# Turned probabilities of both heads in one tile, joint copies for the two small chunks and the packed rows, and one inversion of a pair's nine sums

## The chip, the cores and the metric

The kernel runs on one core of one Trainium2 chip. The metric is the device time of one execution in microseconds. Three runs of the kernel before took 829.68, 830.39 and 831.4 us, median 830.39. One more execution was profiled; its own time was 829.02 us, and its span, from the first to the last recorded instruction, 827.3 us.

The engines are called PE (matrix products and transposes; PEld is its loading of weights, which overlaps the products), DVE, ACT, POOL and SP. Each runs its own instructions in their order and waits on semaphores for the others. The large transfers are issued from SP's queue.

## The reference

First causal attention over 8 batches, 8 heads, 576 positions and a head size of 64, with a bias that is the difference of running sums; its output is then the input of a mixture of 8 experts, of which each token takes one.

```python
s_pos = np.maximum(s, 0.0)
cum = np.cumsum(s_pos, axis=-1)
bias = -(cum[:, :, :, None] - cum[:, :, None, :])
scores = np.where(causal, -1000000000.0, scores + np.minimum(bias, 0.0))
scores = scores - np.max(scores, axis=-1, keepdims=True)
attn = np.exp(scores)
attn = attn / (np.sum(attn, axis=-1, keepdims=True) + 1e-09)
return np.matmul(attn, v).astype(np.float32)
...
h = np.maximum(x[mask] @ w1[e], 0.0)
out[mask] = gate_w[mask, None] * (h @ w2[e])
```

There are 4608 tokens of 512 numbers; an expert has 1024 hidden units.

## The kernel before

**Tiling.** Attention works on 32 pairs. A pair is one head of two batches; the code calls the two `ab` 0 and 1, and the title calls them both heads. The 576 queries of each are cut in four chunks of 128 and a rest of 64; the rests of both batches are packed into one chunk of 128 rows. So a pair has nine chunks: `i` from 0 to 7 (`ab = i // 4`, chunk `c = i % 4` with `128 * (c + 1)` keys), and `i = 8`, the packed rows, with 576 keys. They are taken in the order 3, 7, 2, 6, 8, 1, 5, 0, 4 (`ORDER`).

**A chunk's way.** PE makes the scores in two products into one bank `sp` (four buffers): `KA` by `QH` (L373) and `KB` by `QL` (L395); the packed rows take L408 and L409 in two halves of 288 keys. DVE adds the mask, takes the minimum and writes `pe` or `pep` to SBUF (L397, L411). ACT takes the exponential in place, with the row's sum into `sums` (L417). Three steps later (`LAG`) PE turns the probabilities in blocks of 128x128 into a PSUM tile `pt` (L427; packed rows L440), of which there are **two buffers**, and a copy puts them into `PT` in SBUF: ACT at L430 for `i < 8`, DVE at L446 for the packed rows. The fifth block of the packed rows goes to a corner of the tile `o`.

**A pair's end.** `tail` runs twice. With `g = 1`: PE multiplies the turned probabilities of the queries from 256 on by V (L467, 20 products in all); this needs the chunks 2 and 3 and the packed rows. ACT and DVE copy the result into `oT` (L470, L474), PE projects it by `pw` and `pq` (L347), and DVE scales it by the inverted sums `rs` (L489, L491). With `g = 0` the same is done for the queries 0 to 255, that is chunks 0 and 1. `rs` is made by an addition on ACT (L479) and a reciprocal on DVE (L480), once for each `g`.

**Order of the work.** The loop in `run` writes steps in program order, one chunk per step, and the turning of chunk k - 3 behind the scores of chunk k. A scheduler then fixes the order on each engine from its own estimates; some `issue_after` edges hold it. POOL makes the exact high and low parts of the next pair's keys and queries meanwhile. After every eighth pair `done` routes the tokens that are complete: the sums of the gate columns (L670, DVE) and what follows run in the steps `QUIET` of the next pairs.

**Experts.** From about 380 us on PE multiplies gathered tokens by the expert weights (L1081, L1056) to the end.

**Tiles that the change touches.** `PT`: three tiles of 128x1984, of which a pair takes two in turn. `oT`: two tiles. `pe`: six buffers of 128x512. `V`: three buffers, loaded one pair ahead.

Of the kernel before, what the change touches and what calls it, by code (L numbers as in the profile page):

```python
# [7 lines left out]
F32 = mybir.dt.float32  # L8
# [3 lines left out]
AF = mybir.ActivationFunctionType  # L12
ALU = mybir.AluOpType
# [24 lines left out]
class Attn:  # L38
# [3 lines left out]
    def __init__(self, ctx, tc, qkv, s, ident, wg):  # L42
        nc = tc.nc
# [10 lines left out]
        self.QL = [t[:, :1280].rearrange("p (a x) -> p a x", a=2) for t in self.QLx]  # L54
        self.KA = [c.tile([P, 2, KW], F32R, name=f"KA{u}") for u in range(2)]
        self.KB = [c.tile([P, 2, KW], F32R, name=f"KB{u}") for u in range(2)]
        self.PT = [c.tile([P, PTW], F32, name=f"PT{u}") for u in range(3)]
        self.oT = [c.tile([P, 640], F32, name=f"oT{u}") for u in range(2)]
        self.pw = c.tile([P, 8, 2 * XW], F32, name="pw")
        self.pq = c.tile([P, 8, XW], F32, name="pq")  # L60
        self.mk = c.tile([P, 800], F32, name="mk")
# [4 lines left out]
        self.hold, self.act, self.sp = [None], None, None  # L66
        self.t1 = ExitStack()
        t1 = self.t1p = self.t1.enter_context(tc.tile_pool(name="cst", bufs=1, side="right"))
        sr = t1.tile([P, KW], F32, name="sr")
        for k in HALVES:  # L70
            nc.sync.dma_start(sr[:, k], s[:, k])
        raw = self.raws()
# [18 lines left out]
        s8 = t1.tile([P, KW], F32, name="s8")  # L91
# [198 lines left out]

    def consts(self):
        nc = self.nc
        for u in range(2):
            nc.gpsimd.memset(self.oT[u][:, 512:], 0.0)
        for t in self.PT:
            nc.vector.memset(t[64:, PTW - 64:], 0.0)

    def raws(self):
        return [self.ld.tile([P, 2, KW], F32, name="rawq"), self.ld.tile([P, 2, KW], F32, name="rawk")]
# [6 lines left out]
        return raw  # L306

    def load_v(self, pi):
        V = self.ld.tile([P, 2, 5, 64], F32, name="V", bufs=3)
        self.nc.sync.dma_start(V, self.qkv[pi, :, 4 * KW:].rearrange("p (a j d) -> p a j d", a=2, j=5))  # L310
        return V

# [63 lines left out]
    def score(self, st, i):  # L376
        nc = self.nc
# [4 lines left out]
        if i < 8:  # L382
# [1 line left out]
            n = P * (c + 1)  # L384
            nn = max(n, 256)
            q0 = 704 * ab + P * c
            t = self.wk.tile([P, 512], F32, name="pe", bufs=6)
            if st["pi"] == 0 and not st["s"]:

                for j in ORDER[:SPB]:  # L390
# [27 lines left out]

    def trans(self, st, i):
        nc = self.nc  # L420
        pe, PT = st["s"].pop(i), st["PT"]
        cp = nc.vector.tensor_copy if i in PTDVE else nc.scalar.copy
        if i < 8:
            ab, c = i // 4, i % 4
            pt = self.ps1.tile([P, 512], F32, name="pt")
            for j in range(c + 1):
                self.pe.append(nc.tensor.transpose(out=pt[:, P * j:P * j + P], in_=pe[:, P * j:P * j + P], identity=self.ident).ins)  # L427
            v = min(P * c, 320)
            w = PT[ab][:, P * c - v:P * c - v + PTS * (c + 1)].rearrange("p (j s) -> p j s", s=PTS)
            cp(w[:, :, v:v + P], pt[:, :P * (c + 1)].rearrange("p (j q) -> p j q", q=P))  # L430
        else:
            for j0, nj in ((0, 4), (4, 1)):
                if nj == 4:
                    pt = self.ps1.tile([P, 512], F32, name="pt")
                else:
                    st["o"] = self.ps2.tile([P, 512], F32, name="o")
                    pt = st["o"][:64, 384:]
                kp = P if nj == 4 else 64
                for j in range(nj):
                    self.pe.append(nc.tensor.transpose(out=pt[:kp, P * j:P * j + P], in_=pe[:, P * (j0 + j):P * (j0 + j) + kp], identity=self.ident).ins)  # L440
                for ab in range(2):
                    if nj == 4:
                        w = PT[ab][:, 128:128 + 4 * PTS].rearrange("p (j s) -> p j s", s=PTS)[:, :, 384:]
                    else:
                        w = PT[ab][:kp, PTW - 64:].unsqueeze(1)
                    cp(w, pt[:kp, :P * nj].rearrange("p (j a q) -> p a j q", a=2, q=64)[:, ab])  # L446

    def tail(self, st, g):

        nc = self.nc  # L450
        V, PT, x, h = st["V"], st["PT"], st["x"], st["h"]
        for _ in range(TD + g):
            yield
        q0, q1 = (256, KW) if g else (0, 256)
        o = st["o"] if g else self.ps2.tile([P, 512], F32, name="o")
        oT = self.oT[st["pi"] % 2]

        pe, self.pe = self.pe, []
        nj = 5 if g else 2
        for j in range(nj):  # L460
            f = max(P * j, q0)
            for ab in range(2):
                r = slice(64 * ab, 64 * ab + 64)
                with ExitStack() as after:
                    for i in pe:
                        after.enter_context(self.tc.issue_after(i))
                    m = nc.tensor.matmul(o[r, f - q0:q1 - q0], V[:, ab, j, :], PT[ab][:, PTS * j + f if j < 4 else PTW - 64:PTS * j + q1 if j < 4 else PTW], start=j == 0, stop=j == nj - 1)  # L467
            pe = [m.ins]
        self.wall = m.ins
        nc.scalar.copy(oT[:, q0:q0 + 256], o[:, :256])  # L470
        if g:
            for ab in range(2):
                r = slice(64 * ab, 64 * ab + 64)
                nc.vector.tensor_copy(oT[r, 512 + 64 * ab:576 + 64 * ab], o[r, 256:320])  # L474
        yield
        n = 5 if g else 4
        rs = self.sm.tile([P, 5], F32, name="rs")
        with self.tc.issue_after(self.hold[0]), self.tc.issue_after(self.act):
            nc.scalar.activation(rs[:, :n], st["sums"][:, 4 * g:4 * g + n], AF.Identity, bias=self.eps[:, :1])  # L479
            nc.vector.reciprocal(rs[:, :n], rs[:, :n])  # L480
        xo = self.xo
        for u in range(2):
            c = 2 * g + u
            self.pw_(xo[:, 2 * XW * u:2 * XW * u + 2 * XW], oT[:, P * c:P * c + P], self.pw[:, h, :], start=True, stop=True)
        if g:
            self.pw_(xo[:, 4 * XW:5 * XW], oT[:, 512:], self.pq[:, h, :], start=True, stop=True)
        src = xo[:, :4 * XW].rearrange("p (t d) -> p t d", t=4)
        rv = rs[:, :4].unsqueeze(2).broadcast_to([P, 4, XW])
        nc.vector.tensor_tensor(x[g][:, :, :, h], src.rearrange("p t (d r) -> p t d r", r=2), rv.rearrange("p t (d r) -> p t d r", r=2), ALU.mult)  # L489
        if g:  # L490
            nc.vector.tensor_scalar(x[2][:, 0, :, h], xo[:, 4 * XW:5 * XW].rearrange("p (d r) -> p d r", r=2), rs[:, 4:5], None, ALU.mult)  # L491

    def run(self, npair, newx, done, setup):

# [4 lines left out]
        for k in range(n + LAG + 9):  # L499
            if k < n:  # L500
# [885 lines left out]
```

## Time and profile before

| | |
|---|---|
| median of three runs | 830.39 us (829.68 to 831.4) |
| profiled execution | 829.02 us, its span 827.3 us |
| PE busy | 812.1 us, 98% of the span |
| DVE, ACT busy | 545.6 us (66%), 541.3 us (65%) |
| POOL busy | 360.5 us (44%) |

The page lists busy time by engine; the view by windows gives it by stretch; the timeline lists instructions with start and length, in brackets the idle time just ahead of them and what ended it. Consecutive matmuls overlap in the records (a product of 0.48 us can be followed by the next after 0.31 us), so PE can stand as busy while it waits. What a wait costs is then read from the distance of the starts, not from the busy time.

### The profile page before, as it was taken

Reading aid. Unit: us, or ns where it says so; the run is one execution under the profiler, and the core shown is the slowest. Engines: PE = TensorE matmul, PEld = TensorE weight load, DVE = VectorE, ACT = ScalarE, POOL = GpSimd, SP = SyncE. Lnnn points to the kernel's source line nnn. Section 1 sums busy time; section 2 is a strip of 40 time slices with the busy share of each in tenths; the row PEclk is TensorE's granted clock in tenths of the full one; section 3 lists DMA queues with packets and bytes.
Section 4 is the critical chain, followed back from the end, with each engine's and each line's share of the span. In section 5 each row is a group of like instructions: output and inputs, shape, how many; then the busy total and the mean of one; then the engine's idle time right before and its main releaser. Section 6 shows DMA issues by size and latency. Waiting matters only on the chain. (4 is left out here: it accounts for less than half of the span.)

```text
span 827.3 us, 16879 instructions
## 1 busy us (share of the span) xinstructions
PE 812.1 (98%) x5692; PEld 695.5 (84%) x5692; DVE 545.6 (66%) x1502; ACT 541.3 (65%) x1292; POOL 360.5 (44%) x384
## 2 busy tenths in 40 slices
PE   7999999999999999999999999999999999999997
PEld 6778877877887878887888899998888999988884
DVE  7666667667666677766489865555666656555874
ACT  6788888888888888885365554444455555444663
POOL 8959768988689867992501000000000000000001
PEclk9999999999999999999999999999999999999999
DMA  7665555866567657738697866655556776555970
GB/s 238 187 195 180 180 179 181 254 223 195 170 182 230 208 155 213 226 97 288 222 381 291 312 259 257 229 202 197 213 201 244 258 258 243 199 202 207 380 247 28
DMA packets 68549, 182.31 MB, mean 220 GB/s; under 512 B 7993, under 2 KB 8889, under 8 KB 68334
## 3 DMA queue, kind: packets, MB, share of 16 engines
q1 hardware_dynamic: 62622, 161.17, 57.5%
q0 software_dynamic: 5840, 20.06, 6.3%
q8 instruction: 45, 0.74, 0.4%
q14 instruction: 42, 0.34, 0.1%
HBM read 144.73 MB, written 26.80 MB: 207 GB/s over the span
## 5 line engine op out<-in xcount | busy, mean ns | idle before, releaser
L1067 POOL DMA_INDIRECT out<-ys,oi x36 | 36.5, 1015 | 368.6 <-ACT ys L1066 297.5
L397 DVE CUSTOM_DVE_ANT_0 pe<-sp,mk 128x512 f32<-128x512 f32 (+3 forms) x256 | 121.2, 487 | 63.2 <-PE sp L395 55.5
L417 ACT ACTIVATE pe<-pe,mx 128x512 f32<-128x512 f32 (+3 forms) x256 | 143.8, 562 | 22.4 <-DVE mx L397 21.0
L427 PE MATMUL pt<-ident,pe 128*128 128x128 f32 x640 | 117.7, 281 | 4.0 <-ACT PT L430 2.8
L430 ACT COPY PT<-pt 128x512 f32<-128x512 f32 (+3 forms) x256 | 106.3, 416 | 13.3 <-PE pt L427 12.6
L1083 ACT ACTIVATE hT<-hp 128x512 fp32r<-128x512 f32 x72 | 42.8, 595 | 93.1 <-PE hp L1081 92.6
L467 PE MATMUL o<-PT,V 128*64 128x320 f32 (+4 forms) x896 | 100.7, 364 | 0.0
L373 PE MATMUL sp<-KA,QH 128*128 128x256 f32 (+2 forms) x256 | 97.3, 389 | 2.5 <-POOL KA L236 2.5
L427 PEld LDWEIGHTS pt<-ident,pe 128*128 128x128 f32 x640 | 75.4, 141 | 26.8 <-ACT PT L430 11.2
L467 PEld LDWEIGHTS o<-PT,V 128*64 128x64 f32 x896 | 58.7, 136 | 41.0 <-issue 9.4
L1081 PE MATMUL hp<-xT,wcb 128*128 128x256 f32 x648 | 89.6, 282 | 0.0
L395 PE MATMUL sp<-KB,QL 76*128 76x256 f32 (+2 forms) x256 | 88.4, 349 | 0.0
L1081 PE MATMUL hp<-xT,wca 128*128 128x256 f32 x624 | 87.3, 282 | 0.5 <-ACT xT L1033 0.5
L327 POOL TENSOR_TENSOR KA<-rawk,KA 64x576 fp32r<-64x576 f32 x62 | 87.0, 1419 | 0.2
L327 POOL TENSOR_TENSOR QL<-rawq,QH 64x576 fp32r<-64x576 f32 x62 | 86.6, 1413 | 0.2
L1084 DVE SCALAR_TENSOR_TENSOR hT<-hp,hT 128x512 fp32r<-128x512 f32 x72 | 49.5, 687 | 55.1 <-ACT hT L1083 54.9
L1081 PEld LDWEIGHTS hp<-xT,wcb 128*128 128x128 f32 x648 | 83.1, 188 | 0.6
L1081 PEld LDWEIGHTS hp<-xT,wca 128*128 128x128 f32 x624 | 80.4, 188 | 1.4 <-issue 0.7
L1056 PE MATMUL y<-wcb,hT 128*128 128x512 f32 x336 | 81.2, 398 | 0.0
L1056 PEld LDWEIGHTS y<-wcb,hT 128*128 128x128 f32 x336 | 62.7, 188 | 14.7
L1081 PE MATMUL hp<-xT,wcc 128*128 128x256 f32 x456 | 64.6, 281 | 0.0
L1056 PE MATMUL y<-wca,hT 128*128 128x512 f32 x264 | 63.9, 398 | 0.0
(285 smaller groups left out, 1611.9 us busy)
## 6 DMA issues: line engine op xcount, KB each, us to landing
wrbw<-in_w SPq DMA_DIRECT2D x104, 512.0 KB
wraw<-in_w SPq DMA_DIRECT2D x56, 512.0 KB
rawq<-in_qkv SPq DMA_DIRECT2D x31, 576.0 KB
rawk<-in_qkv SPq DMA_DIRECT2D x31, 576.0 KB
xg<-lists SPq DMA_DIRECT2D x18, 576.0 KB
V<-in_qkv SPq DMA_DIRECT2D x32, 320.0 KB
KB<-KA SPq DMA_DIRECT2D x62, 144.0 KB
lists<-z SPq DMA_DIRECT2D x8, 576.0 KB
```

The source lines that it names most:

```text
L327: self.last = nc.gpsimd.tensor_tensor(o, i, h, ALU.subtract).ins
L373: self.pe.append(self.nc.tensor.matmul(sp[:, :nn], QH[:, q0:q0 + P], self.KA[u][:, ab, :nn], start=True, stop=False).ins)
L395: self.pe.append(nc.tensor.matmul(sp[:, :nn], QL[:EXT, q0:q0 + P], KB[:EXT, ab, :nn], start=False, stop=True).ins)
L397: ins = nc.vector.tensor_tensor_reduce(out=t[:, :n], in0=sp[:, :n], in1=self.mk[:, 512 - n:512], scale=-0.125, scalar=3.0e38, op0=ALU.add, ...
L417: self.act = nc.scalar.activation(t[:, :n], t[:, :n], AF.Exp, bias=m, scale=-1.0, accum_out=st["sums"][:, o:o + 1]).ins
L427: self.pe.append(nc.tensor.transpose(out=pt[:, P * j:P * j + P], in_=pe[:, P * j:P * j + P], identity=self.ident).ins)
L430: cp(w[:, :, v:v + P], pt[:, :P * (c + 1)].rearrange("p (j q) -> p j q", q=P))
L467: m = nc.tensor.matmul(o[r, f - q0:q1 - q0], V[:, ab, j, :], PT[ab][:, PTS * j + f if j < 4 else PTW - 64:PTS * j + q1 if j < 4 else PTW], ...
L1056: self.last[0] = nc.tensor.matmul(y[u], hT[:, a, f, P * u:P * u + P], W[4 + f // 2][:, c, 512 * (f % 2):512 * (f % 2) + 512], start=f == 0 ...
L1081: nc.tensor.matmul(hp[:, u], W[k][:, a, f:f + P], xT[:, c, k], start=k == 0 and i == 0, stop=k == 3 and i == 2)
L1083: hi = nc.scalar.activation(hs, hp, AF.Relu)
L1084: lo = nc.vector.scalar_tensor_tensor(hT[:, 1, 2 * m:2 * m + 2], hp, 0.0, hs.bitcast(F32), ALU.max, ALU.subtract)
```

## The change

`PT` becomes two tiles of `[128, 2, 1984]`, one for each pair in turn, with both `ab` in one tile. That lets one copy serve both: for the chunks 0 and 1 (`JOINT`) the turning of `ab = 0` is left until that of `ab = 1`, both go into one `pt`, and ACT makes one copy of 128x2x2x128 or 128x2x128 in place of two. The packed rows take one DVE copy in place of two, and so does their corner in `o`. `rs` has nine columns and is made once a pair, with `g = 1`. `oT` becomes a single tile, `pe` gets a tile of its own width for each chunk length, with two buffers, `V` has two buffers and its load is written three steps later, and the two scratch tiles of the start lie inside `PT[1]`.

```diff
+JOINT = (0, 1)
...
-        self.PT = [c.tile([P, PTW], F32, name=f"PT{u}") for u in range(3)]
-        self.oT = [c.tile([P, 640], F32, name=f"oT{u}") for u in range(2)]
+        self.PT = [c.tile([P, 2, PTW], F32, name=f"PT{u}") for u in range(2)]
+        self.oT = c.tile([P, 640], F32, name="oT")
...
-        sr = t1.tile([P, KW], F32, name="sr")
+        sr, s8 = (self.PT[1][:, 0, KW * u:KW * u + KW] for u in range(2))
...
-        V = self.ld.tile([P, 2, 5, 64], F32, name="V", bufs=3)
+        V = self.ld.tile([P, 2, 5, 64], F32, name="V")
...
-            t = self.wk.tile([P, 512], F32, name="pe", bufs=6)
+            t = self.wk.tile([P, n], F32, name=f"pe{c}")
...
-        pe, PT = st["s"].pop(i), st["PT"]
+        PT = st["PT"]
         cp = nc.vector.tensor_copy if i in PTDVE else nc.scalar.copy
+        if i in JOINT:
+            return
         if i < 8:
             ab, c = i // 4, i % 4
+            both = i - 4 in JOINT
             pt = self.ps1.tile([P, 512], F32, name="pt")
-            for j in range(c + 1):
-                self.pe.append(nc.tensor.transpose(out=pt[:, P * j:P * j + P], in_=pe[:, P * j:P * j + P], identity=self.ident).ins)
+            n = P * (c + 1)
+            for a in range(1 - both, 2) if ab else (0,):
+                pe = st["s"].pop(4 * a + c)
+                for j in range(c + 1):
+                    o = n * (a if both else 0) + P * j
+                    self.pe.append(nc.tensor.transpose(out=pt[:, o:o + P], in_=pe[:, P * j:P * j + P], identity=self.ident).ins)
...
+            cp(w[:, :, :, v:v + P], pt[:, :n * (1 + both)].rearrange("p (a j q) -> p a j q", a=1 + both, q=P))
...
-                for ab in range(2):
-                    if nj == 4:
-                        w = PT[ab][:, 128:128 + 4 * PTS].rearrange("p (j s) -> p j s", s=PTS)[:, :, 384:]
-                    else:
-                        w = PT[ab][:kp, PTW - 64:].unsqueeze(1)
-                    cp(w, pt[:kp, :P * nj].rearrange("p (j a q) -> p a j q", a=2, q=64)[:, ab])
+                if nj == 4:
+                    w = PT[:, :, 128:128 + 4 * PTS].rearrange("p a (j s) -> p a j s", s=PTS)[:, :, :, 384:]
+                    cp(w, pt[:, :512].rearrange("p (j a q) -> p a j q", a=2, q=64))
+                else:
+                    cp(PT[:kp, :, PTW - 64:], pt[:kp, :P].rearrange("p (a q) -> p a q", a=2))
...
-        n = 5 if g else 4
-        rs = self.sm.tile([P, 5], F32, name="rs")
-        with self.tc.issue_after(self.hold[0]), self.tc.issue_after(self.act):
-            nc.scalar.activation(rs[:, :n], st["sums"][:, 4 * g:4 * g + n], AF.Identity, bias=self.eps[:, :1])
-            nc.vector.reciprocal(rs[:, :n], rs[:, :n])
+        if g:
+            rs = st["rs"] = self.sm.tile([P, 9], F32, name="rs")
+            with self.tc.issue_after(self.hold[0]), self.tc.issue_after(self.act):
+                nc.scalar.activation(rs, st["sums"], AF.Identity, bias=self.eps[:, :1])
+                nc.vector.reciprocal(rs, rs)
+        rs = st["rs"]
...
-                if k % 9 == 2 and 0 < pi < npair - 1:
+                if k % 9 == 5 and 0 < pi < npair - 1:
                     self.V[pi + 1] = self.load_v(pi + 1)
```

In the changed kernel the lines stand elsewhere: the turning of `i < 8` is L433 and its copy L437, that of the packed rows L448 and its copies L451 and L453, the scores are L372 and L394, the products by V L474, and the projections L346.

The scheduler orders the engines anew. The three places that the prediction speaks of follow. The rows name line, operation, tile written and tiles read, and the shape.

PE in a pair of the middle of attention, from the turning of chunk 6 (the first L427 row) to the products by V, before:

```order
L427 MATMUL pt<-ident,pe 128x128 x3
L395 MATMUL sp<-KB_108,QL_104 128x256
L440 MATMUL o<-ident,pep 64x128
L373 MATMUL sp<-KA_106,QH_102 128x256
L395 MATMUL sp<-KB_108,QL_104 128x256
L373 MATMUL sp<-KA_105,QH_101 128x512
L440 MATMUL pt<-ident,pep 128x128 x4
L395 MATMUL sp<-KB_107,QL_103 128x512
L373 MATMUL sp<-KA_105,QH_101 128x512
L427 MATMUL pt<-ident,pe 128x128 x2
L395 MATMUL sp<-KB_107,QL_103 128x512
L427 MATMUL pt<-ident,pe 128x128 x2
```

and changed:

```order
L394 MATMUL sp<-KB_108,QL_104 128x256
L433 MATMUL pt<-ident,pe_2440 128x128 x3
L372 MATMUL sp<-KA_106,QH_102 128x256
L394 MATMUL sp<-KB_108,QL_104 128x256
L448 MATMUL o<-ident,pep 64x128
L372 MATMUL sp<-KA_106,QH_102 128x256
L448 MATMUL pt<-ident,pep 128x128 x4
L394 MATMUL sp<-KB_108,QL_104 128x256
L372 MATMUL sp<-KA_105,QH_101 128x512
L394 MATMUL sp<-KB_107,QL_103 128x512
L433 MATMUL pt<-ident,pe_2481 128x128 x2
L433 MATMUL pt<-ident,pe_2498 128x128 x2
```

The turning of the chunks 1 and 5 (the last two rows) is one group now, with one `pt`, and one KA and KB product of 512 that stood ahead of it follows it. The turning of the packed rows (L440, now L448) stands ahead of one KB product of 256 and one KA product of 512 that it followed before, and that of chunk 6 is one KA product of 256 earlier.

DVE where the first routing begins, before (`PT<-pt` are the copies of the packed rows, L670 the sums of the gate columns, ISA the mask and minimum):

```order
L480 RECIPROCAL rs<-rs 128x4
L446 COPY PT_110<-o 64x64
L489 TENSOR_TENSOR x<-ox,rs 128x144x2
L446 COPY PT_111<-o 64x64
L670 TENSOR_REDUCE ox<-x 128x32
L446 COPY PT_110<-pt 128x4x64
L670 TENSOR_REDUCE ox<-x 128x32
L446 COPY PT_111<-pt 128x4x64
```

and changed:

```order
L497 TENSOR_TENSOR x<-ox,rs 128x144x2
L678 TENSOR_REDUCE ox<-x 128x32
L396 ISA pe_1690,mx<-sp,mk 128x256
L396 ISA mx 128x1
L678 TENSOR_REDUCE ox<-x 128x32
L396 ISA pe_1702,mx<-sp,mk 128x128
L396 ISA mx 128x1
L453 COPY PT_109<-o 64x2x64
L451 COPY PT_109<-pt 128x2x4x64
```

The two sums no longer stand between the copies but ahead of them, between the chunks.

DVE around the copies into `oT` behind the products by V, before:

```order
L474 COPY oT_112<-o 64x64 x2
L397 ISA pe,mx<-sp,mk 128x384
L397 ISA mx 128x1
```

and changed:

```order
L396 ISA pe_2266,mx<-sp,mk 128x384
L396 ISA mx 128x1
L481 COPY oT<-o 64x64 x2
```

The copies stand behind the mask of the next pair's chunk 2 now. On PE the product by `pq` that reads them follows one KA and one KB product of 384 and one turning that came behind it before.

More of the change, by code (lines that the diff above doesn't have):

```diff
@@ L90, in __init__ @@
         self.warm(WARM)
-        s8 = t1.tile([P, KW], F32, name="s8")
         for k in HALVES:
@@ L292, in consts @@
         nc = self.nc
-        for u in range(2):
-            nc.gpsimd.memset(self.oT[u][:, 512:], 0.0)
+        nc.gpsimd.memset(self.oT[:, 512:], 0.0)
         for t in self.PT:
-            nc.vector.memset(t[64:, PTW - 64:], 0.0)
+            nc.vector.memset(t[64:, :, PTW - 64:], 0.0)
     def raws(self):
@@ L361, in start @@
     def start(self, pi, x):
-        st = dict(pi=pi, h=pi % 8, x=x, s={}, high={}, PT=[self.PT[(2 * pi + ab) % 3] for ab in range(2)], V=self.V.pop(pi))
+        st = dict(pi=pi, h=pi % 8, x=x, s={}, high={}, PT=self.PT[pi % 2], V=self.V.pop(pi))
         st["mx"] = self.sm.tile([P, 10], F32, name="mx")
@@ L420, in trans @@
         nc = self.nc
-        pe, PT = st["s"].pop(i), st["PT"]
+        PT = st["PT"]
         cp = nc.vector.tensor_copy if i in PTDVE else nc.scalar.copy
+        if i in JOINT:
+            return
         if i < 8:
             ab, c = i // 4, i % 4
+            both = i - 4 in JOINT
             pt = self.ps1.tile([P, 512], F32, name="pt")
-            for j in range(c + 1):
-                self.pe.append(nc.tensor.transpose(out=pt[:, P * j:P * j + P], in_=pe[:, P * j:P * j + P], identity=self.ident).ins)
+            n = P * (c + 1)
[4 more added lines that the diff above has]
+                    self.pe.append(nc.tensor.transpose(out=pt[:, o:o + P], in_=pe[:, P * j:P * j + P], identity=self.ident).ins)
             v = min(P * c, 320)
-            w = PT[ab][:, P * c - v:P * c - v + PTS * (c + 1)].rearrange("p (j s) -> p j s", s=PTS)
-            cp(w[:, :, v:v + P], pt[:, :P * (c + 1)].rearrange("p (j q) -> p j q", q=P))
+            h = slice(0, 2) if both else slice(ab, ab + 1)
+            w = PT[:, h, P * c - v:P * c - v + PTS * (c + 1)].rearrange("p a (j s) -> p a j s", s=PTS)
+            cp(w[:, :, :, v:v + P], pt[:, :n * (1 + both)].rearrange("p (a j q) -> p a j q", a=1 + both, q=P))
         else:
+            pe = st["s"].pop(i)
             for j0, nj in ((0, 4), (4, 1)):
@@ L455, in tail @@
         o = st["o"] if g else self.ps2.tile([P, 512], F32, name="o")
-        oT = self.oT[st["pi"] % 2]
+        oT = self.oT
         pe, self.pe = self.pe, []
@@ L466, in tail @@
                         after.enter_context(self.tc.issue_after(i))
-                    m = nc.tensor.matmul(o[r, f - q0:q1 - q0], V[:, ab, j, :], PT[ab][:, PTS * j + f if j < 4 else PTW - 64:PTS * j + q1 if j < 4 else PTW], start=j == 0, stop=j == nj - 1)
+                    m = nc.tensor.matmul(o[r, f - q0:q1 - q0], V[:, ab, j, :], PT[:, ab, PTS * j + f if j < 4 else PTW - 64:PTS * j + q1 if j < 4 else PTW], start=j == 0, stop=j == nj - 1)
             pe = [m.ins]
@@ L487, in tail @@
         src = xo[:, :4 * XW].rearrange("p (t d) -> p t d", t=4)
-        rv = rs[:, :4].unsqueeze(2).broadcast_to([P, 4, XW])
+        rv = rs[:, 4 * g:4 * g + 4].unsqueeze(2).broadcast_to([P, 4, XW])
         nc.vector.tensor_tensor(x[g][:, :, :, h], src.rearrange("p t (d r) -> p t d r", r=2), rv.rearrange("p t (d r) -> p t d r", r=2), ALU.mult)
         if g:
-            nc.vector.tensor_scalar(x[2][:, 0, :, h], xo[:, 4 * XW:5 * XW].rearrange("p (d r) -> p d r", r=2), rs[:, 4:5], None, ALU.mult)
+            nc.vector.tensor_scalar(x[2][:, 0, :, h], xo[:, 4 * XW:5 * XW].rearrange("p (d r) -> p d r", r=2), rs[:, 8:9], None, ALU.mult)
     def run(self, npair, newx, done, setup):
```

## The prediction

> **What bounds the kernel now.** I read the page's busy times, then the view by windows, then the weight loads' waits, then the timeline of single pairs. Page and windows (us, busy time and count of each engine, granted clock, DMA):
>
> ```profile
> span 827.3 us, 16879 instructions
> PE 812.1 (98%) x5692; PEld 695.5 (84%) x5692; DVE 545.6 (66%) x1502; ACT 541.3 (65%) x1292; POOL 360.5 (44%) x384
> ...
> 160.00:320.00 160.00, 159.42 (x1260) 128.42 (x1259) 110.13 (x476) 133.73 (x438) 130.88 (x129) 1.00 0.64 196
> 400.00:800.00 400.00, 400.00 (x2582) 362.66 (x2582) 255.59 (x347) 206.74 (x260) 38.92 (x39) 1.00 0.69 252
> ```
>
> PE is the bound in both halves: 159.42 of 160 us in attention, 400 of 400 in the experts. ACT, whose work the change cuts most, is busy 133.73 of 160 us there (84%) and waits for PE in between. So the change is worth what it takes from PE's stalls, and since the experts are PE from end to end, each microsecond by which attention ends sooner should be kept to the end. These stalls hardly show as idle time; the weight loads' waits from 60 to 370 us show where they sit (sum, times, longest):
>
> ```profile
> PEld pt L427 <- ACT PT L430: 7.2, 30, 0.5
> PEld pt L427 <- PE pt L427: 4.2, 15, 0.3
> ```
>
> The turned tile `pt` has two buffers, and the turning waits until a copy has emptied one. These 11.4 us overlap running products in part, so they bound from above what this wait can cost there. One pair closely, PE first, then DVE, then the pair before it, PE:
>
> ```profile
> 159.22 0.38 PE L427 MATMUL pt<-ident,pe 128*128 128x128 f32 x2
> ...
> 159.85 0.41 PE L427 MATMUL pt<-ident,pe 128*128 128x128 f32 x2
> 160.19 2.27 PE L467 MATMUL o<-PT,V 128*64 128x320 f32 x20
> ...
> 158.95 0.75 DVE L446 COPY PT<-pt 128x256 f32<-128x256 f32 x2
> ...
> 148.04 0.38 PE L427 MATMUL pt<-ident,pe 128*128 128x128 f32 x2
> ...
> 148.49 0.40 PE L395 MATMUL sp<-KB,QL 76*128 76x512 f32 x1
> 148.72 0.38 PE L427 MATMUL pt<-ident,pe 128*128 128x128 f32 x2
> 149.04 0.76 PE L467 MATMUL o<-PT,V 128*64 128x320 f32 x4
> ```
>
> At 148 us nothing is late: two turnings and a product of 512 take 0.45 us (148.04 to 148.49), a product of 512 alone up to the next turning 0.23, and the turning takes 0.32 to the products by V. At 159 the same stretch takes 0.63 and 0.34: 0.20 us lost. It ends with the second copy of the packed rows (158.95 + 0.75 = 159.70; the turning starts 0.15 later, which is what a release takes to become a start). That is the stall of an ordinary pair: 0.20 of the 11.15 us from one product by V (149.04) to the next (160.19).
>
> **The change part by part.** PE's own work stays the same, product by product; only stalls can change.
>
> *Ordinary pairs, what goes.* The turning of chunk 5 no longer waits for the packed rows' second copy: its tile is now that of chunk 6, which ACT empties before. 0.20 us goes.
>
> *Ordinary pairs, what comes.* The order on PE puts the packed rows' turning (`pep`) and chunk 6's earlier. In the kernel before, the pair whose products by V start at 149.04 has nearly this order already and shows the price, PE and then ACT:
>
> ```profile
> 145.47 0.49 PE L427 MATMUL pt<-ident,pe 128*128 128x128 f32 x3
> 145.72 0.36 PE L373 MATMUL sp<-KA,QH 128*128 128x256 f32 x1
> 145.92 0.28 PE L395 MATMUL sp<-KB,QL 76*128 76x256 f32 x1
> 146.03 0.54 PE L427 MATMUL pt<-ident,pe 128*128 128x128 f32 x3
> 146.32 0.36 PE L373 MATMUL sp<-KA,QH 128*128 128x256 f32 x1
> ...
> 146.88 0.28 PE L395 MATMUL sp<-KB,QL 76*128 76x256 f32 x1
> 147.08 0.66 PE L440 MATMUL pt<-ident,pep 128*128 128x128 f32 x4
> 147.49 0.48 PE L373 MATMUL sp<-KA,QH 128*128 128x512 f32 x1
> ...
> 146.36 0.29 ACT L479 ACTIVATE rs<-sums,eps 128x4 f32<-128x4 f32 x1
> 146.55 0.47 ACT L430 COPY PT<-pt 128x384 f32<-128x384 f32 x1
> ```
>
> Chunk 6's turning takes 0.29 us where chunk 2's takes 0.25: 0.04 lost. `pep` starts 0.20 behind a product of 256 that otherwise takes 0.11 (145.92 to 146.03), and takes 0.41 where four turnings at the rate of three (0.25 / 3 each) take 0.33 and, with a first one that is always a little longer, say 0.36: 0.09 and 0.05, together 0.14 lost. It waits for ACT's copy of chunk 2 (146.55 + 0.47 = 147.02). That is 0.18 in all, so this order alone gains next to nothing over 0.20. In the changed kernel `pep` is one product of 256 (0.11) earlier still, and the copy it waits for is earlier by the `rs` that is gone ahead of it (146.55 - 146.36 = 0.19). So 0.14 + 0.11 - 0.19 = 0.06 at `pep`; with 0.04 at chunk 6, 0.10. Bounds: 0 if ACT comes sooner still; 0.04 + 0.14 + 0.11 = 0.29 if ACT's chain doesn't move up.
>
> The `pq` product comes on top. On DVE the copies into `oT` now stand behind a mask of 384 columns, and on PE `pq` stands behind two products of 384 and a turning more:
>
> ```profile
> L397 DVE CUSTOM_DVE_ANT_0 pe<-sp,mk 128x384 f32<-128x384 f32 x28 | 15.6, 557 | 7.4 <-PE sp L395 7.0
> 163.67 0.42 PE L373 MATMUL sp<-KA,QH 128*128 128x384 f32 x1
> 164.11 0.60 PE L427 MATMUL pt<-ident,pe 128*128 128x128 f32 x4
> ```
>
> The copies are later by up to 0.56, `pq` by 164.11 - 163.67 = 0.44 and a turning of about 0.09. A stall between 0 and 0.12; I take 0.06. The new sum is 0.16 against 0.20, a gain of 0.04 a pair (bounds: 0.20 less 0, and 0.20 less 0.41, so +0.20 to -0.21).
>
> *The larger copies.* A joint ACT copy is longer than a single one, and the packed DVE copy too. Neither has a row; these bound them:
>
> ```profile
> L430 ACT COPY PT<-pt 128x512 f32<-128x512 f32 x28 | 15.8, 564 | 0.0
> L430 ACT COPY PT<-pt 128x256 f32<-128x256 f32 x30 | 10.9, 363 | 3.2 <-PE pt L427 3.1
> ```
>
> On ACT, 512 columns take 0.56 in place of 2 x 0.36, off the path. On DVE the copy lies between one of 256 and the two, which take 0.75; I take 0.65, so V's products get the packed rows no later than before. The V load, one pair ahead by its issue, and the smaller buffers cost nothing by this reckoning: a pair's V lands while the 11 us of the pair before run.
>
> *The pair behind each of three group ends.* There L670 stands between the two packed copies (the order above), and the second copy is later by its length:
>
> ```profile
> 204.01 0.48 PE L395 MATMUL sp<-KB,QL 76*128 76x512 f32 x1
> 204.72 0.44 PE L427 MATMUL pt<-ident,pe 128*128 128x128 f32 x2 [0.23 <-ACT PT L430]
> 205.09 0.49 PE L467 MATMUL o<-PT,V 128*64 128x320 f32 x2
> ```
>
> 0.71 + 0.37 against 0.31 (0.45 less the 0.14 of the two turnings ahead) + 0.32: 0.45 lost. With the sums ahead of the copies I give it the ordinary 0.16, a gain of 0.29; the two pairs behind, where routing still crowds DVE, I put at 0.1 together for the group. Three groups: 1.2 us (bounds 0 and 2).
>
> *The first four pairs.* There chunk 5's turning directly follows chunk 1's, both buffers in use:
>
> ```profile
> 23.02 0.41 PE L427 MATMUL pt<-ident,pe 128*128 128x128 f32 x2 [0.47 <-DVE PT L446]
> 34.33 0.38 PE L427 MATMUL pt<-ident,pe 128*128 128x128 f32 x2
> 34.98 0.41 PE L427 MATMUL pt<-ident,pe 128*128 128x128 f32 x2 [0.27 <-DVE PT L446]
> 46.37 0.44 PE L427 MATMUL pt<-ident,pe 128*128 128x128 f32 x2 [0.46 <-ACT PT L430]
> 58.18 0.44 PE L427 MATMUL pt<-ident,pe 128*128 128x128 f32 x2 [0.46 <-ACT PT L430]
> ```
>
> At 34 us the two starts are 0.65 apart where two turnings take about 0.22, so 0.43 is lost, 0.16 more than the idle time in brackets, because the record of a turning outlasts its slot. With 0.16 added to each the four lose 2.3 us. One joint tile cannot wait for itself; less 4 x 0.16 of the ordinary new stalls, the gain is 1.7 (bounds 0.8 and 2.3).
>
> *The last pair* has the same two waits:
>
> ```profile
> 372.75 0.44 PE L427 MATMUL pt<-ident,pe 128*128 128x128 f32 x2 [0.21 <-ACT PT L430]
> 373.64 0.44 PE L427 MATMUL pt<-ident,pe 128*128 128x128 f32 x2 [0.46 <-ACT PT L430]
> 374.01 0.76 PE L467 MATMUL o<-PT,V 128*64 128x320 f32 x4
> ```
>
> With the joint tile the four turnings start at 372.75 and V's products about 0.4 to 0.55 later, at 373.2 to 373.3: 0.7 us (bounds 0.3 and 0.9).
>
> *The sum.* 32 pairs less 4, 3 and 1 are 24 ordinary ones: 24 x 0.04 = 1.0; with 1.2, 1.7 and 0.7 it is 4.6 us. 829.02 - 4.6 = 824.4 for a profiled execution (1.7 us of it around the span, which the change leaves alone); the median lies 1.4 above that execution, so 825.8.
>
> **A rule that speaks against the change.** The Trainium skill, page "Perfetto Trace Analysis", section "Optimizing Scalar/DVE Operations", says that grouping into larger operations can pay where the engine is saturated, and that where it isn't but makes others wait, breaking instructions up may let work finish sooner. ACT at 84% and DVE at 69% of the attention window (133.73 and 110.13 of 160) are of the second kind, and PE waits for both. The trace agrees with both halves of its condition. By this rule alone the joint copies lose; the slower rival below is that case.
>
> **The rivals.**
>
> *No change.* PE's stalls only move: new waits of 0.25 a pair take the place of 0.20. For it: the pair at 145 us, whose new order gains nothing. Against: its `rs` at 146.36, which goes. 24 x -0.05 = -1.2, group ends 0, start 2.3 - 4 x 0.25 = 1.3, end 0.7: a gain of 0.8, 829.6.
>
> *Slower: `pep` waits for the tile of chunk 2.* Its place moved ahead of a KA product of 512 and a KB product of 256, and if ACT's chain ahead of that copy is paced by DVE's masks of the packed rows rather than by ACT's own length, dropping `rs` moves nothing. Then 0.29 at `pep` and chunk 6 and 0.12 at `pq`: 0.41, a loss of 0.21 a pair. 24 x 0.21 = 5.0, nothing at the group ends, against 2.3 - 4 x 0.41 = 0.7 at the start and 0.7 at the end: 3.6 slower, 834.0. It decides from a new stall of 0.28 a pair on, where 24 pairs lose as much as start and end gain, and from 0.34 on a measurement would tell it. For it: ACT is idle in 26 of the window's 160 us, so it isn't always the pace. Against: from 145 us on, `rs` and the copy run back to back on ACT.
>
> *All stalls go.* 24 x 0.20 = 4.8, with 2.0, 2.3 and 0.9: 10.0, 820.4. Against: chunk 6's wait has no reason to go.
>
> *ACT sets the pace.* A pair saves 2 x 0.36 - 0.56 = 0.16 at each of two joint copies and 0.19 of `rs`: about 0.5, 31 pairs 16 us, 814. Against: PE at 159.42 of 160.
>
> **How the numbers follow.** Forecast 0.52, no change 0.21, slower 0.15, all stalls gone 0.11, ACT's pace 0.01. A measurement tells about 0.2% (1.7 us) from no change. The forecast's own range is 823 to 828.5 (a gain of the ordinary pair of 0.14, and of -0.07), wholly on the faster side of 828.7; the forecast, the last two and a little of the second give faster 0.66, same 0.19, slower 0.15. The range runs from 821.0 to 831.5: below it lies some 0.08, above it the larger part of the slower case.
>
> **What would show it.** Right: the distance between V's first products of ordinary pairs falls from 11.15 to about 11.11; no bracketed idle time at the joint turning in the first pairs and the last; waits of the weight load for `pt` fall from 11.4 to some 6 us and move to `pep`; the experts' stretch keeps its length. Wrong: `pep` starting over 0.2 us behind the KA product ahead of it, or `pq` waiting for `oT` in every pair, or an experts' stretch that grows by what attention gave.

## The result and the profile after

The changed kernel took 833.25 us (median of 8 runs, 831.71 to 835.18) against 829.77 us of the kernel before (8 runs, 829.05 to 831.4): a ratio of 1.0043, 95% interval 1.0031 to 1.0055. It is slower by 3.5 us where 4.6 us of gain were forecast. The profiled execution took 832.43 us.

The page's first lines and its windows after (columns as before):

```profile
span 830.6 us, 16652 instructions
PE 814.3 (98%) x5692; PEld 698.1 (84%) x5692; DVE 539.6 (65%) x1405; ACT 530.5 (64%) x1196; POOL 360.3 (43%) x383
...
40.00:60.00 20.00, 17.34 (x132) 13.77 (x130) 11.13 (x45) 13.60 (x43) 14.01 (x18) 1.00 0.64 186
60.00:80.00 20.00, 19.69 (x138) 14.89 (x140) 11.28 (x44) 14.21 (x42) 13.78 (x19) 0.91 0.49 157
...
160.00:320.00 160.00, 160.00 (x1266) 130.55 (x1266) 107.56 (x433) 129.84 (x398) 133.16 (x131) 1.00 0.66 202
400.00:800.00 400.00, 400.00 (x2582) 362.72 (x2581) 255.00 (x348) 206.28 (x260) 41.48 (x41) 1.00 0.69 252
```

ACT has 11 us less to do and DVE 6, as the change says, and PE has none of it. One place stands out: from 40 to 60 us PE is busy for 17.34 of 20 us. The kernel before has this row there:

```profile
40.00:60.00 20.00, 19.07 (x146) 14.86 (x146) 13.22 (x57) 16.25 (x52) 10.50 (x10) 1.00 0.68 217
```

The starts of V's first product in each pair, read from the timeline, say which pairs it is (us from one to the next; the pairs are counted from 0):

| pair | 1 | 2 | 3 | 4 | 5 | ordinary | last |
|---|---|---|---|---|---|---|---|
| before | 11.50 | 11.88 | 11.82 | 11.17 | 11.17 | 11.17 | 11.34 |
| changed | 11.23 | 12.32 | 14.53 | 12.27 | 11.61 | 11.16 | 10.54 |

By the start of pair 5's product the changed kernel is 4.2 us behind (85.58 against 81.35, the first and second row below); at the last pair's it is 2.6 behind (376.59 against 374.01), so 1.7 came back between. The experts' products take the same time, to 0.03 us, and the last write lands 0.7 later behind the last product (7.1 us against 6.4; other runs here have 6.5 to 6.9).

```profile
81.35 0.49 PE L467 MATMUL o<-PT,V 128*64 128x320 f32 x2
```
```profile
85.58 0.49 PE L474 MATMUL o<-PT,V 128*64 128x320 f32 x2
```

What PE waits for there, in the view of waits from 34 to 86 us of the changed kernel, and the timeline of PE (timelines are shown here and below with rows in between left out):

```profile
PE sp L372 <- POOL KA L326: 3.1, 5, 1.9
...
58.94 0.50 PE L372 MATMUL sp<-KA,QH 128*128 128x512 f32 x1 [1.91 <-POOL KA L326]
60.31 0.61 PE L372 MATMUL sp<-KA,QH 128*128 128x512 f32 x1 [0.43 <-POOL KA L326]
```

PE waits for POOL's low part of the next pair's keys. POOL in turn starts late. The chain is on SP's queue; first the kernel before, POOL and then SP (SPq rows are the issue of transfers):

```profile
33.87 1.31 POOL L323 TENSOR_SCALAR KA<-rawk 128x576 fp32r<-128x576 f32 x2 [0.45 <-DMA rawk<-in_qkv]
...
26.24 0.57 SPq L310 DMA_DIRECT2D V<-in_qkv  x1
26.87 0.44 SPq L305 DMA_DIRECT2D rawq<-in_qkv  x1
...
33.57 0.57 SPq L262 DMA_DIRECT2D KB<-ek  x1
```

and the changed kernel, with SP's waits from 20 to 85 us:

```profile
37.67 1.31 POOL L322 TENSOR_SCALAR KA<-rawk 128x576 fp32r<-128x576 f32 x2 [4.75 <-PE sp L394]
...
30.28 0.33 SPq L309 DMA_DIRECT2D V<-in_qkv  x1
30.66 0.42 SPq L304 DMA_DIRECT2D rawq<-in_qkv  x1
...
37.03 0.57 SPq L262 DMA_DIRECT2D KB<-ek  x1
...
SPq L309 <- PE o L474: 10.0, 3, 3.9
```

The load of V stands at the same place of the queue in both. With three buffers it goes out at once; with two it has to wait until PE has multiplied by the V of the pair before last, and three such loads wait 10.0 us in all. Behind it stand the raw keys and queries, the rows that are saved to DRAM (five transfers that take some 5 us to issue) and the next pair's placements into KB and QL. They all go out 3.5 to 4 us later, and so does what POOL makes of them: it starts 6.5 us behind the issue of the raw keys in both kernels (27.35 to 33.87 and 31.14 to 37.67), though the second row names a product of PE as what ended the wait.

The ordinary pair, at last, in the timelines of PE, ACT and DVE of the changed kernel:

```profile
186.93 2.27 PE L474 MATMUL o<-PT,V 128*64 128x320 f32 x20
190.78 0.44 PE L346 MATMUL ox<-pq,oT 128*128 128x72 f32 x2
192.55 0.87 PE L474 MATMUL o<-PT,V 128*64 128x256 f32 x8
196.00 0.66 PE L448 MATMUL pt<-ident,pep 128*128 128x128 f32 x4
197.09 0.60 PE L433 MATMUL pt<-ident,pe 128*128 128x128 f32 x4
198.09 0.76 PE L474 MATMUL o<-PT,V 128*64 128x320 f32 x4
...
195.48 0.47 ACT L437 COPY PT<-pt 128x384 f32<-128x384 f32 x1
...
189.79 0.56 DVE L396 CUSTOM_DVE_ANT_0 pe<-sp,mk 128x384 f32<-128x384 f32 x1 [2.06 <-PE sp L394]
190.27 0.45 DVE L481 COPY oT<-o 64x64 f32<-64x64 f32 x2
```

From V's products with `g = 1` to those with `g = 0` it is 5.62 us, and from there to the next pair 5.54. Measured between the blocks (from the last product of one to the first of the next; medians of the later pairs), the first stretch went from 3.48 to 3.58 and the second from 5.04 to 4.94. The packed rows' turning starts as soon as ACT has copied chunk 2 (195.48 + 0.47 = 195.95), with little lost; and `pq` starts when DVE has made the copies into `oT` (190.27 + 0.45 = 190.72), which stand behind the mask. What the pair wins at one place it loses at the other, to 0.01 us.

### The profile page after: what moved, and what is told of

Read it like the earlier page. It is cut to its first block, busy times and chain, and to the rows that moved or that the text cites. A ratio compares the mean times of both kernels' runs of the same rounds, so it can differ in the third digit from the quotient of the medians.

```text
span 830.6 us, 16652 instructions
## 1 busy us (share of the span) xinstructions
PE 814.3 (98%) x5692; PEld 698.1 (84%) x5692; DVE 539.6 (65%) x1405; ACT 530.5 (64%) x1196; POOL 360.3 (43%) x383
## 5 line engine op out<-in xcount | busy, mean ns | idle before, releaser
L437 ACT COPY PT<-pt 128x512 f32<-128x512 f32 (+1 forms) x192 | 97.1, 509 | 23.3 <-PE pt L433 23.3
L433 PE MATMUL pt<-ident,pe 128*128 128x128 f32 x640 | 111.2, 280 | 0.3
L372 PE MATMUL sp<-KA,QH 128*128 128x256 f32 (+2 forms) x256 | 102.6, 403 | 5.2 <-POOL KA L326 3.3
L474 PE MATMUL o<-PT,V 128*64 128x320 f32 (+4 forms) x896 | 101.8, 367 | 0.0
L474 PEld LDWEIGHTS o<-PT,V 128*64 128x64 f32 x896 | 59.1, 137 | 47.7 <-issue 15.8
L433 PEld LDWEIGHTS pt<-ident,pe 128*128 128x128 f32 x640 | 76.8, 144 | 12.6 <-issue 5.3
L394 PE MATMUL sp<-KB,QL 76*128 76x256 f32 (+2 forms) x256 | 85.5, 337 | 1.5 <-DMA QL<-ek 1.5
L322 POOL TENSOR_SCALAR KA<-rawk 128x576 fp32r<-128x576 f32 x60 | 39.3, 671 | 58.2 <-PE sp L372 25.0
```

What stands on the lines that cost most here:

```text
L372: self.pe.append(self.nc.tensor.matmul(sp[:, :nn], QH[:, q0:q0 + P], self.KA[u][:, ab, :nn], start=True, stop=False).ins)
L394: self.pe.append(nc.tensor.matmul(sp[:, :nn], QL[:EXT, q0:q0 + P], KB[:EXT, ab, :nn], start=False, stop=True).ins)
L433: self.pe.append(nc.tensor.transpose(out=pt[:, o:o + P], in_=pe[:, P * j:P * j + P], identity=self.ident).ins)
L437: cp(w[:, :, :, v:v + P], pt[:, :n * (1 + both)].rearrange("p (a j q) -> p a j q", a=1 + both, q=P))
```

## The experiments

Theory Q: two V buffers make V's load wait on SP's queue, and all behind it. Theory P: something else of the new tiles (PT in two, the scratch in it, one oT) costs the start. Times are medians; ratios are to the kernel before (829.7 to 829.9 us beside these runs).

**Three V buffers again** (e1).

```diff
-        V = self.ld.tile([P, 2, 5, 64], F32, name="V")
+        V = self.ld.tile([P, 2, 5, 64], F32, name="V", bufs=3)
...
-            t = self.wk.tile([P, KW], F32, name="pep", bufs=2)
+            t = self.wk.tile([P, KW], F32, name="pep", bufs=1)
```

> The changed kernel with three V buffers again; pep gets one buffer in place of two, which makes the room (its next writer comes nine steps later); PE's order is that of the changed kernel. Theory Q (queue): with two V buffers the load of V on SP's queue waits for the products by V of the pair before last, and what stands behind it (the raw keys and queries, the saved rows, the next pair's placements) comes late; this made the five pairs up to the products at 85.6 us lose 4.2 us, and gone it gives 833.3 - 4.2 - about 0.7 = 828 to 829, with these products at about 81 us. Theory P (PT of two tiles, scratch inside PT, one oT tile): nothing changes, 833.

829.23 us, ratio 0.9995 (0.9986 to 1.0005). Pair 5's product starts at 80.52, 5.1 us earlier than in the changed kernel and 0.8 earlier than in the kernel before; SP waits for V's products nowhere from 20 to 85 us. Theory P falls: every other tile but `pep` is as changed, and the two runs that follow change V alone.

Not all that the start gained lasts. At pair 3 this run is 1.64 ahead of the kernel before (57.38 against 59.02), but from there to pair 4 it takes 11.97 us in place of 11.17. PE comes sooner, while POOL starts on the next keys at 60.22 as in the kernel before (60.08), so PE waits for them:

```profile
68.69 0.50 PE L372 MATMUL sp<-KA,QH 128*128 128x512 f32 x1 [0.54 <-POOL KA L326]
```

The time is still only that of the kernel before, above all because another 2.2 us went in one later pair (13.33 us from pair 10 to pair 11 where others take 11.16). Its PE and POOL:

```profile
147.88 0.50 PE L372 MATMUL sp<-KA,QH 128*128 128x512 f32 x1 [1.44 <-POOL KA L326]
...
142.44 1.20 POOL L732 DMA_INDIRECT lists<-x,di  x1 [5.24 <-ACT pe L416]
143.67 2.80 POOL L326 TENSOR_TENSOR QL<-rawq,QH 64x576 fp32r<-64x576 f32 x2
146.43 2.77 POOL L326 TENSOR_TENSOR KA<-rawk,KA 64x576 fp32r<-64x576 f32 x2
```

The first scatter of routed tokens stands ahead of the next pair's low parts on POOL, waits there for 5.24 us, and PE waits for the low parts behind it. The changed kernel has that order too and loses 0.6 us by it in the same pair; the kernel before has the scatter behind the low parts.

**Two V buffers in the kernel before** (e2).

```diff
-        V = self.ld.tile([P, 2, 5, 64], F32, name="V", bufs=3)
+        V = self.ld.tile([P, 2, 5, 64], F32, name="V", bufs=2)
```

> The kernel before with two V buffers in place of three and nothing else; PE's order is the same. Theory Q: the start loses what the changed kernel lost, 3 to 5 us, 833 to 835, and the ordinary pairs keep their 11.16. Theory P: 829.8, no change.

836.92 us, ratio 1.0089 (1.0064 to 1.0115): 7 us slower by this one number, more than expected. In its profiled execution, the shortest of four (834.4), pair 5's product starts at 85.22 in place of 81.35, and the waits from 20 to 85 us are those of the changed kernel:

```profile
SPq L310 <- PE o L467: 8.9, 3, 3.8
...
PE sp L373 <- POOL KA L327: 2.6, 6, 0.9
```

The clock stays at 1.00 there, so these 3.9 us are waits alone. The ordinary pairs keep 11.16. The load of V was written at step 2 there, as before, so it is the buffers and not the later step that make it wait.

**Two V buffers, V's load written at step 8** (e3).

```diff
-                if k % 9 == 5 and 0 < pi < npair - 1:
+                if k % 9 == 8 and 0 < pi < npair - 1:
                     self.V[pi + 1] = self.load_v(pi + 1)
```

> The changed kernel with its two V buffers, but the load of V written three steps later (step 8 of a pair in place of 5), so that on SP's queue it stands behind the raw loads and the saved rows. Theory Q: those no longer wait behind it, most of the 4.2 us comes back, 828.5 to 830. If two buffers cost by a late V itself, and not by the queue, the start stays as slow or gets slower: 833 or more.

826.02 us, ratio 0.9953 (0.9936 to 0.9970): 7.2 us faster than the changed kernel and faster than before, better than expected. Now the raw loads and the saved rows go out ahead of V. Pair 5's product starts at 79.98, and the scheduler also put the scatter later on POOL, where it waits 0.18 us in place of 5.24, so the pair at 147 us takes 11.16. A late V by itself costs nothing here; to have others wait behind it does.

**DVE's copies into `oT` first** (e4; on e1, so with three V buffers).

```diff
+                self.otc = nc.vector.tensor_copy(oT[r, 512 + 64 * ab:576 + 64 * ab], o[r, 256:320]).ins
...
+            with self.tc.issue_after(self.otc) if self.otc is not None else ExitStack():
+                ins = nc.vector.tensor_tensor_reduce(out=t[:, :n], in0=sp[:, :n], in1=self.mk[:, 512 - n:512], scale=-0.125,
```

> As e1, and DVE's two copies into oT are put ahead of the mask of the next pair's chunk 2; PE then has pq right behind the pw products, as in the kernel before. Theory Q with the second half (the ordinary pair gains 0.105 at the packed rows and loses the same 0.105 at pq): the stretch from V's products with g = 1 to those with g = 0 goes from 3.58 back to 3.48, the pair from 11.16 to about 11.06, 28 pairs give 2.9 us on e1: about 825.5. Rival: the 0.105 is no wait but the new place of the products on PE, or the packed rows' gain goes with it: the pair stays at 11.16 and the time at that of e1.

831.54 us, ratio 1.0021 (1.0011 to 1.0031): slower than e1. The first stretch fell, to 3.53 only, and the second rose from 4.94 to 5.08; the pair takes 11.26. PE and ACT of one pair:

```profile
193.84 0.66 PE L450 MATMUL pt<-ident,pep 128*128 128x128 f32 x4
194.71 0.66 PE L435 MATMUL pt<-ident,pe 128*128 128x128 f32 x4
...
191.58 0.59 ACT L439 COPY PT<-pt 128x512 f32<-128x512 f32 x1 [0.20 <-PE pt L435]
192.06 0.78 ACT L418 ACTIVATE pep<-pep,mx 128x576 f32<-128x576 f32 x1
193.32 0.47 ACT L439 COPY PT<-pt 128x384 f32<-128x384 f32 x1
194.19 0.47 ACT L439 COPY PT<-pt 128x384 f32<-128x384 f32 x1
```

Both turnings start right at the end of a copy (193.32 + 0.47 = 193.79, 194.19 + 0.47 = 194.66). The scheduler had moved PE's and ACT's order with the edge: ACT takes the copy of chunk 7 ahead of the packed rows' exponential here, for which it idles 0.20 us, and all its copies behind come later. The wait for POOL behind the scatter, at 146 us, is there as in e1.

**The joint copies, one at a time** (both on e3; first e5, with none, then e6, with chunk 1 alone).

```diff
-JOINT = (0, 1)
+JOINT = ()
```

> As e3 (V late, 826.0 us), but no joint copies for the chunks 0 and 1 (each turned and copied by itself); packed rows, rs and tiles stay as changed. PE's order then has pq right behind the pw products again and the packed rows' turning behind the KA product of 512. Theory J (the joint copy of chunk 0 is what puts the mask ahead of the oT copies on DVE and so costs 0.1 at pq): V's products with g = 1 to g = 0 back at 3.48 in place of 3.57. The stretch behind, 4.94 in e3, stays there if its gain came from the one rs and the packed copy (time 823 to 824.5), and goes back to 5.04 if it came from joining chunk 1 (time 826). Rival: 3.57 stays, it is the place of the products and not the copies.

830.75 us, ratio 1.0005 (0.9995 to 1.0015); 3.53 and 5.08: the first stretch fell, but the second rose above both values that were expected, and the time is almost 5 us above the higher of the two that were given for it.

```diff
-JOINT = (0, 1)
+JOINT = (1,)
```

> As e3, but only chunk 1 is joint. Theory J: 3.48 at pq, as in e5. The stretch behind the products with g = 0 keeps 4.94 if the packed rows' turning finds its tile empty (823 to 824.5), or goes to about 5.08 as in e4, where this turning had the same place and waited for ACT (827 to 828).

828.89 us, ratio 0.9991 (0.9975 to 1.0007); 3.53 and 5.08. So chunk 0's joint copy does put the mask ahead of the `oT` copies: without it `pq` follows `pw` and the first stretch falls, though to 3.53 and not to 3.48. But the second stretch takes e4's form with it. Both, and e4, have the same order on ACT; joining chunk 1 made no difference to it.

**The sums inverted twice a pair again** (e7, on e3).

```diff
-        if g:
-            rs = st["rs"] = self.sm.tile([P, 9], F32, name="rs")
...
+        with self.tc.issue_after(self.hold[0]), self.tc.issue_after(self.act):
+            nc.scalar.activation(rs[:, 4 * g:4 * g + n], st["sums"][:, 4 * g:4 * g + n], AF.Identity, bias=self.eps[:, :1])
```

> As e3, but the inverse sums are made twice a pair again (five columns with g = 1, four with g = 0). The prediction's step: the rs of g = 0 stood on ACT ahead of the copy of chunk 2 for which the packed rows' turning waits. If so the stretch behind g = 0 goes from 4.94 to 5.0 to 5.1, 28 pairs, 2 to 4 us slower than e3: 828 to 830. Rival: that copy has slack in this order and nothing is lost, 826.

828.67 us, ratio 0.9985 (0.9974 to 0.9996), 2.7 us above e3. The second stretch is 5.00 in place of 4.94, the pair 11.23. ACT, and the turning that waits:

```profile
190.64 0.29 ACT L488 ACTIVATE rs<-sums,eps 128x4 f32<-128x4 f32 x1
190.82 0.47 ACT L437 COPY PT<-pt 128x384 f32<-128x384 f32 x1
...
191.34 0.66 PE L448 MATMUL pt<-ident,pep 128*128 128x128 f32 x4
```

The turning starts 0.05 behind the copy's end (191.29). Without this second `rs` the copy starts 0.18 sooner behind V's products (2.93 us behind the first of them in the changed kernel, 3.11 here). The pair gains only 0.06 of that, since the scheduler puts a KB product of 256 ahead of the waiting turning here, which follows it there.

**The packed rows copied in two pieces again** (e8, on e3).

```diff
-                    cp(w, pt[:, :512].rearrange("p (j a q) -> p a j q", a=2, q=64))
+                    v = pt[:, :512].rearrange("p (j a q) -> p a j q", a=2, q=64)
+                    for ab in range(2):
+                        cp(w[:, ab], v[:, ab])
```

> As e3, but the packed rows' turned tile is copied in two pieces again (one for each head); PE's order is that of e3. The prediction's step: with chunks 1 and 5 in one tile nothing on PE waits for the second copy, so the time stays within 0.7 us of e3's 826.0. Rival: the joint DVE copy itself was the gain, and the pair goes back up by 0.1 to 0.2: 829 to 831.

827.18 us, ratio 0.9969 (0.9956 to 0.9982); 3.58 and 4.94, the pair 11.17. Median 1.2 above e3, more than the 0.7 allowed, but none of it is in the pairs: the profiled execution is 0.98 behind e3's already at pair 0's product (24.11 against 23.13) and 1.04 at the last pair's. The two intervals overlap. On PE's path the joint packed copy does nothing.

**ACT's order held.** The copy of chunk 7 is put behind the packed rows' exponential, alone or (e9) with the edge of e4; e9 is on e3, e10 on e6 and e11 on e5.

```diff
-            cp(w[:, :, :, v:v + P], pt[:, :n * (1 + both)].rearrange("p (a j q) -> p a j q", a=1 + both, q=P))
+            with self.tc.issue_after(self.act) if i == 7 else ExitStack():
+                cp(w[:, :, :, v:v + P], pt[:, :n * (1 + both)].rearrange("p (a j q) -> p a j q", a=1 + both, q=P))
```

> As e3 (joint copies of chunks 0 and 1, V late) with two edges of order: DVE's copies into oT ahead of the mask of the next pair's chunk 2 (as in e4), and ACT's copy of chunk 7 behind the exponential of the packed rows, as e3 and the kernel before have it and e4 had not. Theory J: e4 won 0.05 at pq and lost 0.14 in the stretch behind g = 0 because ACT took the exponential late there and so the copies of chunks 2 and 6 came 0.3 late. With the order mended the first stretch is 3.48 to 3.53 and the second 4.94 or below: a pair of 11.0 to 11.06, 821.5 to 823.5. Rival: it is the place of the packed rows' turning on PE that costs in e4 (behind the KA product of 512, as here again): 5.08 stays, 828 to 829.

> As e6 (only chunk 1 joint) with the edge on ACT alone. Theory J as in e9: 3.48 to 3.53 and 4.94 or below, 822 to 825 (e6 lost another 0.4 in the fifth pair). Rival: as e6, 829.

> As e5 (no joint chunk) with the edge on ACT alone. Theory J: 3.48 to 3.53 and 4.94 or a little above, since chunk 5's turning has a tile of its own to wait for again; e5's loss in the first three pairs (14.3 and 12.8 us in place of 11.3) may stay, then 825 to 827, otherwise 822 to 824. Rival: joining chunk 1 is what keeps the second stretch short, then it goes above 5.0 and the time to 829 or more.

| | median us | ratio (95%) | stretches | pair |
|---|---|---|---|---|
| e9, chunks 0 and 1 joint | 823.77 | 0.9928 (0.9908 to 0.9948) | 3.53, 4.86 | 11.04 |
| e10, chunk 1 joint | 823.50 | 0.9920 (0.9899 to 0.9942) | 3.53, 4.85 | 11.03 |
| e11, none joint | 826.98 | 0.9961 (0.9947 to 0.9975) | 3.53, 4.92 | 11.10 |

The pair came below 11.16 at last. e10, PE and ACT of the second stretch:

```profile
189.56 0.60 PE L449 MATMUL pt<-ident,pep 128*128 128x128 f32 x4
189.92 0.48 PE L394 MATMUL sp<-KB,QL 76*128 76x512 f32 x1
190.24 0.62 PE L433 MATMUL pt<-ident,pe 128*128 128x128 f32 x4
...
187.08 0.78 ACT L416 ACTIVATE pep<-pep,mx 128x576 f32<-128x576 f32 x1
187.85 0.56 ACT L438 COPY PT<-pt 128x512 f32<-128x512 f32 x1
188.82 0.46 ACT L438 COPY PT<-pt 128x384 f32<-128x384 f32 x1
```

The packed rows' turning has the place that e4 gave it, and finds its tile empty since 189.28: the four take 0.36 us and nothing waits. So e4's loss was ACT's order and not the place; chunk 6's turning stands one KA product of 256 later than in e4 and e6, as in the kernel before. e10 and e9 are the fastest here, 0.8% and 0.7% ahead of the kernel before. With no chunk joint the second stretch is 0.07 longer: this is what joining chunk 1 is worth in an ordinary pair, once nothing else is in its way. The first three pairs gain about 0.5 each by it and the last 0.4, and from pair 3 to pair 4 e10 gives 1.0 back to the wait for POOL. Joining chunk 0 as well is worth nothing that these runs can tell.

## Why the prediction was wrong

**The step that failed** is the sentence that "the V load, one pair ahead by its issue, and the smaller buffers cost nothing by this reckoning". It asked whether V lands in time, and V does. It did not ask what stands behind the load on SP's queue while it waits for a buffer. That wait is 10.0 us, and what follows it cost the start about 5 us: pair 5's product is at 85.58 with two buffers and 80.52 with three, the other tiles but `pep` the same. One number in the kernel before does the same (e2), and an order of the queue mends it (e3).

**A second term was put at nothing**: POOL. The gain of 1.7 us forecast for the first four pairs was there with three buffers (1.64, e1), but half of it went again in the next pair, where PE waits for POOL's low part of the keys, and 0.83 was left at pair 5. Two V buffers turned it into a loss of 4.2.

**The slower rival** had the time (834.0 against 833.25) and not the mechanism. The ordinary pair lost nothing: 11.16 against 11.17, where it asked for 0.21 a pair. Nor did the rule decide that the Trainium skill has in its page "Perfetto Trace Analysis", section "Optimizing Scalar/DVE Operations" (where an engine isn't saturated but holds others up, smaller operations may let work finish sooner): e10 joins chunk 1 and is faster by 0.07 a pair than e11, which joins none.

**The steps that held.** Chunk 5's wait is gone. The new waits at chunk 6 and at the packed rows were put at 0.04 and 0.06, so that the second stretch should fall by 0.10; it fell by 0.105. In the pair shown above they are 0.05 (chunk 6's turning takes 0.30 up to the next product, chunk 2's 0.25) and 0.06 (the packed rows' turning starts 0.01 late and takes 0.41 where 0.36 was reckoned). The one `rs` moves ACT's copy by the 0.18 that the sum had at 0.19.

**The term that was too small** in an ordinary pair is `pq`. It was put at 0.06, bounded by 0.12; the first stretch grew by 0.105, and so the 24 ordinary pairs gave 0 in place of 1.0 us. About 0.05 of it goes when the copies into `oT` stand ahead of the mask again (e4, e5, e6); what makes the rest stays open. `pq` waiting for `oT` in every pair was one of the prediction's signs of being wrong. Its sign of being right in the weight loads' waits misled: those for `pt` fell from 11.4 us to 0.5, further than the 6 that were expected, and the ordinary pair got no shorter.

**The other terms.** The group ends were put at 1.2: the second and third group won 0.5 each, the first lost 0.2 to the scatter on POOL, together 0.8. The last pair was put at 0.7 and won 0.8. The experts did keep what attention gave. Summed from rows: start -4.2, the rest of attention +1.7, the last write -0.7, which is, but for rounding, the span's 3.3. What makes the last write later stays open.

With the queue mended (e3) the median is 826.02, close to the 825.8 that were forecast, and that is partly luck. Its profiled execution is 3.2 us shorter than the one before: 0.7 stands ahead of pair 0's product, where the forecast has nothing; 0.7 comes from there to pair 5, 0.05 from the ordinary pairs, 1.5 from the group ends and 0.8 from the last pair; the last write takes back 0.5.

**No change**, the rival that made 0.25 of 0.20, was as near for the ordinary pairs as the forecast with its 0.16: the new waits add up to about 0.21 (0.05, 0.06 and 0.105). **All stalls go** was not: the mended order (e10) reaches 11.03, 0.14 a pair below before, and there about 0.05 is still lost in the first stretch. **ACT's pace** is out: 11 us less of ACT moved nothing by itself.

## What to carry to other kernels

When a buffer is taken away, ask not only whether its data still come in time, but which queue its load stands in and what is behind it there: an early load with no free buffer stopped everything behind it in its queue, and the same load written later cost nothing. Where a scheduler orders the work, a change that frees time on one engine is worth what the new order makes of it; compare the orders of all engines around each wait, and hold the one place that matters with an edge. A sum over waits may be right to 0.05 us a pair and still lose to one transfer that no row of the old trace shows waiting.

## What the runs showed of the hardware

A stall of PE can cost more than itself. In the changed kernel PE stands from about 57.0 to 58.9 us and again at 60 us for POOL's keys, and the granted clock then falls to half for about 3.4 us (windows of the changed kernel; the last three numbers are clock, DMA share and GB/s):

```profile
59.00:60.00 1.00, 0.88 (x5) 0.56 (x5) 0.00 (x0) 0.09 (x1) 1.00 (x1) 1.00 1.06 399
60.00:61.00 1.00, 0.69 (x2) 0.59 (x3) 0.00 (x0) 0.89 (x3) 0.26 (x1) 0.78 1.09 406
...
63.00:64.00 1.00, 1.00 (x8) 0.41 (x6) 0.00 (x0) 0.70 (x2) 0.48 (x1) 0.51 0.13 48
64.00:65.00 1.00, 1.00 (x14) 0.64 (x10) 0.00 (x0) 0.00 (x0) 1.00 (x3) 1.00 0.01 3
```

V's 20 products in these microseconds take 3.16 us where every other pair's take 2.05, so at least about 1.1 of the 5 us are the clock's. The Trainium skill, page "TensorE: Matmul & The Clock Gate", Part 1, tells of half rate after an idle window of about 3.4 us, and as long a busy one to come back. The time to come back agrees with these rows; the drop came here with about 2.3 us of idle time in two pieces.

The length of a gap alone does not decide it. In e4 PE was idle for 2.27 us in one piece (146.43 to 148.70) and the clock stayed at 1.00, as it did in e1 with 1.4 us there. In the 3.41 us ahead of each drop PE was idle for 65% of the time in the changed kernel (57.14 to 60.56 us), and for 62% and 66% in e5 and e9. Any 3.41 us around e4's whole gap would be idle for as much. The readings agree if the clock is decided in fixed slots of 3.41 us: counted on from the clock's change at 14.70 us, e4's gap falls into two of them, idle for 41% and 26%. This is a reading of these traces and was not tested.

In single executions of e5 and e9, the slowest of their runs (833.4 and 829.1 us), the first three pairs took about 5 us longer than e10's. The traces show where it began, DVE of e5 and then of e9:

```profile
32.99 2.91 DVE L618 TENSOR_SCALAR ew<-e 128x8 f32<-128x8 f32 x1
...
34.24 3.74 DVE L619 TENSOR_SCALAR ecap<-e 128x8 f32<-128x8 f32 x1
```

In e10 the same two small operations of the routing take 0.16 and 0.26 us. Here they hold up the masks behind them, those hold up ACT and PE, PE is idle for 2.53 and 3.53 us, and then the clock halves. Both end within 0.07 us of the end of POOL's work on `QH` (35.83 and 37.95), up to which POOL had run without a break; in e10 POOL pauses until 34.36. That POOL held DVE up is argued from this and not shown: no run tests it. Open stays also the wider spread of the runs with two V buffers loaded early (834.4 to 839.2 in e2).
